# A fused convolution and mixture of experts on Trainium2: rows of up to 4 KB in the dispatch's loads, and three loads at a time

## The chip, the cores and the metric

The kernel runs on one core of one Trainium2 chip. The metric is the device time of one execution in microseconds, the median of the runs of a kernel. Five engines work side by side, each on its own queue of instructions: PE (matrix products), DVE and ACT and POOL (elementwise work), and SP, which here only issues DMA transfers. All transfers run on the core's 16 DMA engines. Before the change the median of 3 runs is 889.47 us (888.85 to 889.73).

## What is computed

A long convolution with a gate, whose result is the input of a mixture of experts with soft routing. Shapes: 4 sequences of 11456 positions and 128 channels, so 45824 tokens of 128 channels; 8 experts of 4 slots each; 1024 hidden features.

```python
h_filt = (np.maximum(pos_emb @ w1, 0.0) @ w2) * window
y = irfft(rfft(x * v) * rfft(h_filt))[:, :S, :]      # along the sequence
x = (x * y).reshape(B * S, D)                        # 45824 x 128

logits = x @ phi                                     # 45824 x 32
d = softmax(logits, axis=0)                          # over the tokens
slot_input = (d.T @ x).reshape(8, 4, 128)
slot_out[e] = np.maximum(slot_input[e] @ moe_w1[e], 0.0) @ moe_w2[e]
c = softmax(logits, axis=1)                          # over the 32 slots
out = c @ slot_out                                   # 45824 x 128
```

## The kernel before

**Convolution.** It is computed as a transform in matrix products, in eight groups of 16 channels. The last step of a group gives gated rows of x, which `p4_out` (L462, L465) and `p4_rest` (L471) store to a scratch tensor `scr` in HBM, channels by tokens. `scr` consists of 16 pieces (`_pieces`), most of them 3296 tokens long; inside a piece each channel is one contiguous row. For the last group the steps run over seven sets of rows, t = 0 to 6, and each stores two pieces.

**Blocks.** The mixture works on 23 blocks: 22 of 16 x 128 = 2048 tokens (1 MB, 8 KB on each of 128 partitions) and one of 768. A block in SBUF has one of 11 places of a ring (`NP`), which are parts of tiles that the convolution has left: `ffw` (blocks 0 to 4), `extra` (block 5), `xreg` and `E`. The token blocks are handled in pairs ("units"), twelve of them.

**Loads of x.** `load` (L695) calls `load_tokens`, which cuts a block where a piece of `scr` ends and then into equal parts of at most `RUN` = 450 tokens, and issues one DMA for each part on SP (L709). A part of 410 tokens is 128 rows of 1640 B. `weights` (L657) loads the first 112 channels of blocks 0 to 5 before the last group's rows exist; `ahead` adds their last 16 channels and loads blocks 6 to 10, each behind the stores of the set t that completes it. Blocks 11 to 22 are loaded by `fetch` inside the mixture: `fetch(i)` loads block i + 11 into the place of block i as soon as block i has been transposed.

**Loads of matrices.** There are 16, of 512 KB: `load_weights` issues each as two halves of 128 rows of 2 KB (L676). Matrices 0 and 1 are loaded by `weights`, the other 14 by `fetch(12)` to `fetch(18)`, two in each place that falls free.

**Order on SP.** DMAs go out in the order in which they stand on SP's queue. The scheduler that lays out the program gives each DMA of SP one of eight semaphores in turn, and a DMA waits until the one eight before it has landed. A DMA into a place also waits until that place has been read.

**Dispatch.** For a unit m the loop does: exponentials of the logits on ACT (`exps`, L849, from the PSUM tile `pl`), transposes of two blocks on PE (L722) and their copies out of PSUM on ACT (L728), the transpose of the weights on DVE (L876), the logits of unit m + 1 on PE (L795), their maxima on DVE (L818, L820), the product with the dispatch weights of unit m - 1 (L890), and the running maximum (L837, L839), which the next exponentials need. PSUM holds two `pl` tiles, one for each block of a unit, so the logits of unit m + 1 overwrite what the exponentials of unit m read.

**Experts and output.** Behind the last unit come the experts: `up` (L1078) with matrices 0 to 7, `turn_hidden` (L1086), `down` (L1096) with matrices 8 to 15. Then each of 24 stretches of tokens is multiplied by the result (L1136), copied and stored (L1144) as 128 rows of up to 8 KB.

Of the kernel before, what the change touches and what calls it, by code (L numbers as in the profile page):

```python
# [17 lines left out]
B, S, D = 4, 11456, 128  # L18
# [27 lines left out]
FF = 1024  # L46
# [592 lines left out]
class Moe:  # L639
# [4 lines left out]
    NP = 2 * XB + 1  # L644
    OB = 4
    CB = 8 * NB
    RUN = 450

    def __init__(self, tc, cp, scr, phi, mw1, mw2, rep, out):
        self.tc, self.cp, self.scr, self.out = tc, cp, scr, out  # L650
        self.phi, self.mw1, self.mw2, self.rep = phi, mw1, mw2, rep

        self.blocks = [(q, min(self.NB, QN - q)) for q in range(0, QN, self.NB)]
        self.xt, self.xq, self.wts = {}, {}, []
        self.pieces = sorted(_pieces().values())

    def weights(self):  # L657
# [14 lines left out]

    def load_weights(self, e, place):
        src = (self.mw1, self.mw2)[e // NEXP][e % NEXP]
        for f in range(0, FF, FF // 2):
            self.tc.nc.sync.dma_start(out=place[:, f : f + FF // 2], in_=src[:, f : f + FF // 2])  # L676
        self.wts.append(place)

    def logit_banks(self):
# [21 lines left out]
    def load_tokens(self, t, z0, z1, d0, d1):  # L701
        for a, m in self.pieces:
            lo, end = max(z0, a), min(z1, a + B * m)
            src = self.scr[D * a : D * (a + B * m)].rearrange("(d t) -> d t", d=D)
            n = max(0, end - lo)
            parts = -(-n // self.RUN) if d0 == 0 else min(n, 1)
            cuts = [lo + n * k // parts for k in range(parts + 1)] if parts else []
            for y0, y1 in zip(cuts, cuts[1:]):
                self.tc.nc.sync.dma_start(out=t[d0:d1, y0 - z0 : y1 - z0], in_=src[d0:d1, y0 - a : y1 - a])  # L709

    def turn(self, pool, tag, i, k0, k1, shared=False):
        nc, inorder = self.tc.nc, self.tc.keep_in_program_order
# [529 lines left out]
def _pieces():  # L1242
    out, t = {}, 0
    for rb in ORDER:
        for h in range(2):
            n = PW - (FULL if rb == 0 and h == 0 else 0)
            out[rb, h] = t, n
            t += B * n
    for h in range(2):
        n = 4 * (R // 8 - LEFT // 8) - 1 + h  # L1250
        out["rest", h] = t, n
        t += B * n
    assert t == TOK
    return out
# [49 lines left out]
```

## Time and profile before

| | |
|---|---|
| median of 3 runs | 889.47 us |
| profiled execution, time | 889.77 us |
| profiled execution, span from first to last instruction | 888.0 us |
| PE busy with products | 855.6 us, 96% of the span |
| DVE, ACT, POOL busy | 715.6, 455.0, 393.2 us |
| DMA moved | 197.04 MB in 108195 packets |
| queue of the instruction fetches for PE | 128 packets, 2.10 MB |

The convolution takes the span up to about 734 us, the dispatch to about 815, the experts to 828, the output the rest. The shares of busy time over the whole span hide this: PE is at 96% in the mean, but in the output it waits for copies and stores. A profile's idle pieces carry the name of what ended them. A wait for several things carries the name of the one that came last by the profile; "issue" means that the engine waited for nothing that the profile shows. DMA share is the mean busy share of the 16 DMA engines.

### The profile page before, as it was taken

Reading aid. Unit: us, or ns where it says so; the run is one execution under the profiler, and the core shown is the slowest. Engines: PE = TensorE matmul, PEld = TensorE weight load, DVE = VectorE, ACT = ScalarE, POOL = GpSimd, SP = SyncE. Lnnn points to the kernel's source line nnn. Section 1 sums busy time; section 2 is a strip of 40 time slices with the busy share of each in tenths; the row PEclk is TensorE's granted clock in tenths of the full one; section 3 lists DMA queues with packets and bytes.
Section 4 is the critical chain, followed back from the end, with each engine's and each line's share of the span. In section 5 each row is a group of like instructions: output and inputs, shape, how many; then the busy total and the mean of one; then the engine's idle time right before and its main releaser. Section 6 shows DMA issues by size and latency. Waiting matters only on the chain. (4 is left out here: it accounts for less than half of the span.)

```text
span 888.0 us, 37632 instructions
## 1 busy us (share of the span) xinstructions
PE 855.6 (96%) x16264; PEld 790.4 (89%) x16264; DVE 715.6 (81%) x1239; ACT 455.0 (51%) x971; POOL 393.2 (44%) x538
## 2 busy tenths in 40 slices
PE   9999999999999999999999999999999999989991
PEld 8998989999999999999999999999999987666540
DVE  5967976899799889989988998899779048886791
ACT  5775558315811751483167128414821637986761
POOL 5003860492078019405910960393079013785750
PEclk9999999999999999999999999999999999999996
DMA  9973775558646754775486476557626978999698
GB/s 317 389 237 109 210 229 173 147 155 268 203 126 200 243 167 133 227 237 172 122 269 201 129 225 207 168 173 229 211 71 186 281 191 271 309 302 327 271 417 372
DMA packets 108195, 197.04 MB, mean 222 GB/s; under 512 B 15865, under 2 KB 71371, under 8 KB 105278
## 3 DMA queue, kind: packets, MB, share of 16 engines
q1 hardware_dynamic: 107854, 194.51, 68.8%
q8 instruction: 128, 2.10, 1.0%
q14 instruction: 37, 0.30, 0.1%
q0 software_dynamic: 32, 0.07, 0.0%
q10 hardware_dynamic: 144, 0.07, 0.0%
HBM read 137.73 MB, written 56.86 MB: 219 GB/s over the span
## 5 line engine op out<-in xcount | busy, mean ns | idle before, releaser
L350 POOL TENSOR_TENSOR T<-m 111x256 f32<-111x256 f32 (+1 forms) x199 | 150.8, 758 | 343.7 <-DVE m L344 343.7
L344 DVE TENSOR_TENSOR m<-p,T 111x1024 f32<-111x1024 f32 (+1 forms) x175 | 200.4, 1205 | 12.7 <-POOL T L351 7.2
L360 PE MATMUL p<-tab,T 111*99 111x112 f32 x2048 | 205.2, 260 | 1.3 <-POOL T L351 0.3
L360 PEld LDWEIGHTS p<-tab,T 111*99 111x99 f32 x2048 | 198.8, 170 | 6.1 <-issue 1.6
L340 PE MATMUL p<-T,W 128*64 128x128 f32 (+1 forms) x3168 | 196.9, 276 | 0.2 <-issue 0.2
L425 ACT ACTIVATE vc<-p 128x412 f32<-128x412 f32 (+1 forms) x112 | 51.7, 513 | 265.3 <-PE p L412 219.4
L340 PEld LDWEIGHTS p<-T,W 128*64 128x64 f32 (+1 forms) x3168 | 182.1, 127 | 2.1 <-issue 0.4
L412 PE MATMUL p<-tab,E 99*64 99x103 f32 (+1 forms) x3584 | 174.1, 252 | 1.2 <-DVE E L373 0.6
L412 PEld LDWEIGHTS p<-tab,E 99*64 99x64 f32 x3584 | 166.4, 136 | 3.3 <-ACT vc L425 0.8
L375 ACT ACTIVATE E<-p 99x448 f32<-99x448 f32 x254 | 131.9, 575 | 63.5 <-PE p L360 57.8
L351 POOL TENSOR_TENSOR T<-m 111x256 f32<-111x256 f32 (+1 forms) x199 | 147.4, 741 | 0.0
L186 ACT ACTIVATE T<-p 128x396 f32<-128x396 f32 x240 | 100.3, 536 | 11.6 <-PE p L174 11.5
L174 PE MATMUL p<-tab1x,x 53*64 53x99 f32 x3648 | 86.7, 246 | 0.2 <-ACT E L224 0.2
L174 PEld LDWEIGHTS p<-tab1x,x 53*64 53x64 f32 x3648 | 79.9, 132 | 4.4 <-ACT E L224 0.4
L443 DVE TENSOR_TENSOR p<-p,vc 128x824 f32<-128x824 f32 (+1 forms) x46 | 47.0, 1022 | 9.9 <-ACT vc L425 9.9
L268 DVE TENSOR_TENSOR x<-x,T 128x448 f32<-128x448 f32 x51 | 31.6, 619 | 22.2 <-DMA x<-in_xf_dram 17.8
L274 DVE TENSOR_TENSOR x<-T 128x224 f32<-128x224 f32 x102 | 39.2, 426 | 1.8
L270 DVE TENSOR_TENSOR T<-x 128x224 f32<-128x224 f32 x102 | 39.2, 426 | 1.7
L224 ACT ACTIVATE E<-fl 111x512 f32<-111x512 f32 (+1 forms) x50 | 26.8, 627 | 21.3 <-PE fl L218 21.3
L451 DVE TENSOR_TENSOR E<-p,E 128x824 f32<-128x824 f32 x36 | 36.6, 1017 | 1.2
L728 ACT ACTIVATE xreg<-pt 128x512 f32<-128x512 f32 (+1 forms) x68 | 35.0, 609 | 2.6 <-PE pt L722 2.5
L344 DVE TENSOR_TENSOR m<-p,E 111x1024 f32<-111x1024 f32 (+1 forms) x25 | 28.7, 1202 | 5.1 <-PE p L340 4.9
(162 smaller groups left out, 970.2 us busy)
## 6 DMA issues: line engine op xcount, KB each, us to landing
x<-in_xf_dram SPq DMA_DIRECT2D x114, 256.0 KB, 4.1
out_dram<-xreg SPq DMA_DIRECT2D x16, 1024.0 KB, 10.3
E<-in_xi_dram SPq DMA_DIRECT2D x37, 412.0 KB, 4.3
T<-in_vf_dram SPq DMA_DIRECT2D x65, 224.0 KB, 4.9
scr<-E SPq DMA_DIRECT2D x67, 206.0 KB, 3.8
T<-hs SPq DMA_DIRECT2D x63, 154.0 KB, 4.5
hs<-E SPq DMA_DIRECT2D x12, 784.0 KB, 4.7
mv<-in_vf_dram SPq DMA_DIRECT2D x42, 224.0 KB, 4.5
```

What stands on the lines that cost most here:

```text
L174: inorder(nc.tensor.matmul(ps[h][RP * d : RP * d + RP, i, s, :], lhsT=sd[js, i, s, d, :], rhs=tab1x[js, J * (s + d) : J * (s + d + 1)], st ...
L186: inorder(nc.scalar.activation(dst, src, AF.Copy))
L270: inorder(eng.tensor_tensor(out=vt[:, :, m : m + 2], in0=xr[:, :, 0:2], in1=xr[:, :, 2:4], op=op))
L340: inorder(nc.tensor.matmul(ps[ns, i].rearrange("p b c -> p (b c)"), lhsT=W[:, k0 + i, ns], rhs=Tf[:, :, k0 + i, :], start=True, stop=True, ...
L344: inorder(nc.vector.tensor_mul(m[:, :n].rearrange("p k s e c i -> p k s (e c i)").rearrange("p k s (b c) -> p k s b c", c=CG), ps[:, :n].u ...
L350: inorder(eng.tensor_tensor(out=Ty[:, 0], in0=m[:, :n, 0, 0], in1=m[:, :n, 1, 1], op=ALU.subtract))
L351: inorder(eng.tensor_tensor(out=Ty[:, 1], in0=m[:, :n, 1, 0], in1=m[:, :n, 0, 1], op=ALU.add))
L360: inorder(nc.tensor.matmul(pk[:, i, 2 * s : 2 * s + 2, :].rearrange("p q r -> p (q r)"), lhsT=T[0:N1, s, 2 * k + i, u // 2, :, u % 2], rhs ...
L375: inorder(nc.scalar.activation(dst, src, AF.Copy))
L412: inorder(nc.tensor.matmul(pv[RP * h : RP * h + RP, 2 * k + i, w, j0:], lhsT=E[:J, r, 2 - 2 * w + s, :], rhs=tab4[:, s, o + j0 : o + NJ], ...
L425: inorder(nc.scalar.activation(vc[:, w, :, j0:], pv[:, :, 0, j0:], AF.Copy, scale=2.0 * w - 1.0))
L443: inorder(nc.vector.tensor_tensor(out=pw[:, :, :, j0:], in1=vc[:, :, :, j0:], op=ALU.add, in0=pw[:, 1:2, :, j0:].to_broadcast([128, 2, 4, ...
```

## The change

`RUN` becomes 1024: a load of x has rows of up to 4 KB, so a whole block loads in two or three parts, depending on where pieces of `scr` end. A matrix is loaded in one DMA of 128 rows of 4 KB. Both kinds go through a new function, `paced`: a load is made to wait until the third paced load before it has landed (`OPEN` = 3). Loads of part of the channels and matrices 0 and 1 are not paced and not counted. The wait is one of SP, which issues the load. Nothing else changes.

```diff
-    RUN = 450
+    RUN = 1024
+    OPEN = 3
...
     def load_weights(self, e, place):
         src = (self.mw1, self.mw2)[e // NEXP][e % NEXP]
-        for f in range(0, FF, FF // 2):
-            self.tc.nc.sync.dma_start(out=place[:, f : f + FF // 2], in_=src[:, f : f + FF // 2])
+        self.paced(self.tc.nc.sync.dma_start(out=place, in_=src), e > 1)
         self.wts.append(place)
...
             for y0, y1 in zip(cuts, cuts[1:]):
-                self.tc.nc.sync.dma_start(out=t[d0:d1, y0 - z0 : y1 - z0], in_=src[d0:d1, y0 - a : y1 - a])
+                self.paced(self.tc.nc.sync.dma_start(out=t[d0:d1, y0 - z0 : y1 - z0], in_=src[d0:d1, y0 - a : y1 - a]),
+                           d0 == 0 and d1 == D)
+
+    def paced(self, load, whole=True):
+        if not whole:
+            return
+        if len(self.open) >= self.OPEN:
+            self.tc.add_manual_dep(load.ins, self.open[-self.OPEN], mybir.DependencyInfo(
+                mybir.DependencyClass.Sync, mybir.DependencyReason.DATA), reason="few loads at a time")
+        self.open.append(load.ins.name)
```

## Rows read from the trace of the kernel before

**Rows 1.** Busy time by stage: window, length, each engine's busy us, clock, DMA.

```profile
core 0: us, PE busy (x) PEld busy (x) DVE busy (x) ACT busy (x) POOL busy (x), PEclk, DMA share, GB/s
640.00:734.00 94.00, 93.12 (x1679) 90.75 (x1679) 56.24 (x68) 33.35 (x71) 39.40 (x60) 1.00 0.66 184
...
756.54:797.35 40.81, 37.49 (x875) 25.95 (x876) 34.85 (x65) 37.27 (x81) 33.42 (x38) 1.00 0.96 309
797.35:815.34 17.99, 16.21 (x397) 12.63 (x396) 13.16 (x32) 12.33 (x31) 9.65 (x8) 1.00 1.00 347
...
828.38:888.00 59.62, 40.34 (x258) 18.89 (x254) 37.95 (x69) 32.43 (x61) 23.79 (x37) 0.88 0.96 394
```

**Rows 2.** Timeline of PE: start, length, line, operation, count [idle before, its releaser].

```profile
756.54 1.92 PE L795 MATMUL pl<-xreg,aux 128*32 128x512 f32 x16 [0.70 <-DMA E<-scr]
...
768.38 0.64 PE L890 MATMUL pa<-E,ev 128*32 128x128 f32 x16 [0.52 <-issue]
...
778.77 1.07 PE L795 MATMUL pl<-ffw,aux 128*32 128x512 f32 x8 [0.75 <-DMA extra<-scr]
...
790.72 0.52 PE L722 MATMUL pt<-aux,extra 64*128 64x64 f32 x9 [0.27 <-issue]
791.17 2.24 PE L795 MATMUL pl<-xreg,aux 128*32 128x512 f32 x16
...
797.59 0.24 PE L837 MATMUL pmt<-rd,aux 128*32 128x8 f32 x5 [1.14 <-issue]
...
808.30 0.49 PE L890 MATMUL pa<-E,ev 128*32 128x128 f32 x9 [0.81 <-issue]
...
813.69 0.52 PE L890 MATMUL pa<-xreg,ev 128*32 128x128 f32 x9 [0.42 <-issue]
```

**Rows 3.** Block 15's last part: its issue on SP; size, us to landing.

```profile
773.12 0.39 SPq L709 DMA_DIRECT2D ffw<-scr  x1
...
ffw<-scr SPq DMA_DIRECT2D x1, 205.0 KB, 5.5
```

**Rows 4.** Timeline of ACT ahead of PE's wait at 756.54.

```profile
755.71 0.69 ACT L849 ACTIVATE et<-pl,xreg 128x512 f32<-128x512 f32 x1 [1.49 <-DVE xreg L839]
```

**Rows 5.** Windows between PE's stalls (counts in brackets), and the queue of instruction fetches.

```profile
768.38:790.72 22.34, 20.65 (x504) 14.84 (x504) 19.19 (x38) 20.59 (x47) 18.67 (x23) 1.00 0.94 299
813.69:823.17 9.48, 9.45 (x120) 4.90 (x124) 2.98 (x23) 5.03 (x8) 3.62 (x7) 1.00 0.61 223
...
q8 instruction: 128, 2.10, 1.0%
```

**Rows 6.** DMA packets begun in 795.3 to 795.4 and in 823.8 to 823.9.

```profile
q8 instruction: 1, 0.02, 60.1%
...
q8 instruction: 1, 0.02, 63.8%
```

**Rows 7.** SP's issue at 781.48, and the packet begun in 781.5 to 781.6.

```profile
781.48 1.96 SPq L709 DMA_DIRECT2D xreg<-scr  x1
...
q8 instruction: 1, 0.02, 97.4%
```

**Rows 8.** The DMA issued at 659.95 with nothing queued: size, us to landing.

```profile
E<-in_xi_dram SPq DMA_DIRECT2D x1, 412.0 KB, 3.0
```

**Rows 9.** SP's issues of blocks 6 and 7.

```profile
734.01 5.91 SPq L709 DMA_DIRECT2D xreg<-scr  x10
```

**Rows 10.** Windows of two single rounds and of seven rounds together.

```profile
759.80:766.34 6.54, 6.44 (x155) 4.47 (x152) 5.75 (x11) 6.54 (x15) 4.89 (x6) 1.00 0.99 328
780.91:787.57 6.66, 6.35 (x157) 4.50 (x153) 5.57 (x12) 6.16 (x15) 5.99 (x8) 1.00 0.88 268
...
752.64:802.23 49.59, 45.33 (x1067) 31.83 (x1064) 42.98 (x80) 43.74 (x97) 36.89 (x40) 1.00 0.95 305
```

**Rows 11.** The last half matrix, in issue at 815.5, and its first product.

```profile
xreg<-in_mw_dram SPq DMA_DIRECT2D x1, 256.0 KB, 5.4
...
823.48 1.93 PE L1096 MATMUL pso<-xreg,E 128*32 128x128 f32 x64
```

More of the change, by code (lines that the diff above doesn't have):

```diff
@@ L653, in __init__ @@
         self.blocks = [(q, min(self.NB, QN - q)) for q in range(0, QN, self.NB)]
-        self.xt, self.xq, self.wts = {}, {}, []
+        self.xt, self.xq, self.wts, self.open = {}, {}, [], []
         self.pieces = sorted(_pieces().values())
```

## The prediction

> **What bounds the kernel now.** I read the busy shares by stage first [rows 1]. Up to 734 us the kernel is the convolution, which the change touches only at its end. From 734 to 815 is the dispatch: its loads bring x back from scr, and PE is busy 37.49 of 40.81 us between 756.54 and 797.35 while the DMA engines are at 0.96, and at 1.00 after that. From 828.38 to the end the output goes out at 394 GB/s with the DMA engines at 0.96: that tail is bound by the stores, it starts with the first store, and nothing of the change is in it. So a microsecond won or lost between 734 and 828 is a microsecond of the whole, and nothing else counts.
>
> Next, PE's own order of time in the dispatch, for what ends its idle pieces [rows 2]. Three kinds are seen. (a) The 0.75 us at 778.77 is put down to a load. Block 15's last piece was issued at 773.12 and took 5.5 us [rows 3], so it landed at 778.6, just ahead of the matmul that reads it: a real load wait. The sixteen logits matmuls at 791.17 took 2.24 us instead of the 1.92 us at 756.54 [rows 2]; I take the 0.32 us in their middle as the same thing. Together 1.07 us. (b) The 0.70 us at 756.54 also carries a load's name, but ACT's exponentials, whose bank these matmuls overwrite, run from 755.71 for 0.69 us [rows 4] and end just before: that one is not the loads'. (c) Five idle pieces are put down to "issue": 0.52, 0.27, 1.14, 0.81 and 0.42 us, in all 3.16 us [rows 2].
>
> What (c) is takes one count. Between the stalls at 768.38 and 790.72 PE ran 504 matmuls and 504 weight loads [rows 5]: with some semaphore instructions that is four times 256. The queue of instruction fetches moved 2.10 MB in 128 packets [rows 5], 16.4 KB each, which over 256 instructions is 64 bytes for one. So PE stalls where a new 16 KB of its program begins, because the fetch, which runs on the same DMA engines, is late. How late: after the boundary at 790.72 the fetch for the next block began at 795.3; after 813.69 the next boundary is 120 matmuls on, at 823.17 [rows 5], and the fetch behind that one began at 823.8 [rows 6], when the loads were done. So 4.6 us when loads are queued and 0.7 us when they are not. SP shows the same moment: an issue that cost 0.39 us at 773.12 [rows 3] took 1.96 us at 781.48, with a fetch beginning at 781.5 [rows 7]. Loads and fetches hold each other up.
>
> **The change part by part.**
>
> Rows. Blocks 6 to 22 now load in 91 pieces of mostly 352 to 448 tokens; with 1024 as the limit, and the pieces of scr still cutting them every 3296 tokens, they are 45, of which 12 have the full 4 KB row, 745 tokens or 2.98 KB in the mean. Cost per row: the three stages give 309/0.96 = 322 GB/s at rows of some 1.5 KB, 347 at 2 KB, 394/0.96 = 410 at 8 KB [rows 1]. Over 16 engines that is 94 ns for a row of 2 KB and 320 ns for one of 8 KB, 0.0367 ns a byte between; 2.98 KB then takes 129 ns, which is 371 GB/s. Blocks 11 to 22 are 11.9 MB: 37 us of the engines' time before, 32 after. They were issued in 40.8 us.
>
> The Trainium skill's "DMA: Bandwidth & Descriptors" (section Specifications) gives 512 B as the least transfer for line rate. By that rule rows of 1.5 KB are long enough, the 371 would stay 322, and (a) would not be won. The three stages disagree, 322 to 410 GB/s, though the last one moves stores.
>
> Pace. Loads of blocks 6 and on and of the last 14 matrices wait on SP for the third one before them. Behind a waiting load stand on SP the later loads, and between 734 and 756 also the stores of the last convolution rows to scr. The price is a rate: three loads in each load's latency l. Blocks 11 to 22 are 32 loads, so they take 32 l / 3. From below, a load of 412 KB alone took 3.0 us [rows 8], and 373 KB is the mean here: 32 us, no more than the rows allow. From above, the 5.5 us of a load behind seven others [rows 3]: 59 us. Break-even with the 40.8 us is l = 3.8 us. Three loads queued are 1.1 MB, which the engines at 371 GB/s move in 3.0 us, so I take l = 3.3 us, nearest to the load alone: 35 us, 5 us earlier by block 22 and about 2 by block 15. That takes away (a), 1.07 us: block 15 was only 0.75 late.
>
> The stores between 734 and 756: the ten pieces of blocks 6 and 7 took SP from 734.01 to 739.92 [rows 9]. Now they are five: three go at once, the fourth when the first has landed, 3.3 us on, and the fifth some 0.5 us later. Even with a start 1.5 us late that is 739.3, so the stores behind them find SP free at 740 as before. Taken at nothing; if the first load lands 2 us late, the stores and what is loaded from them are late by up to 2 us.
>
> Fetches. What queues ahead of a fetch falls from eight loads of some 190 KB to three of 373 KB, and for the matrices from eight of 256 KB to three of 512 KB: to 0.75 of the bytes, to 0.38 of the loads. Which of the two counts, the trace does not say; from below, if only the length of a row counts, nothing is won and it gets worse (below); from above all 3.16 us go. Taking bytes, 4.6 us become 3.6, and stalls of under 1 us go; taking loads, all go. I take two thirds, 2.1 us.
>
> Given back. The loop of logits, maxima on DVE, exponentials on ACT and the next logits has a shortest round: a pair of blocks took 6.54 us and 6.66 us where little waited [rows 10]. The seven rounds from 752.64 to 802.23 took 49.59 us [rows 10]; less their five pieces of (a) and (c), 3.0 us, they would take 6.66 each. That is at the floor, so I give back 0.3 us.
>
> At no cost: the 112-partition preloads of blocks 0 to 5 (15 loads instead of 30) and the two first matrices, unpaced, run before 734, where PE is busy 93.12 of 94.00 us [rows 1]: all their waits together, if they had any, are under 0.9 us. The other matrices: the last landed 5.4 us after its issue near 815.5, so by 820.9, and is read at 823.48 [rows 11]; at three times 512 KB in flight they stay bound by the engines, and start earlier. The cover is 2.6 us, of which PE's gain takes most if they did not.
>
> The sum: -1.1 - 2.1 + 0.3 = -2.9 us. The profiled run is 889.77 us with a span of 888.0; the median is 889.47, and I set the sum against it: **886.6 us**.
>
> **Rivals.**
> - *The loads are won, the fetches are not*: the queue ahead of a fetch is measured in neither bytes nor loads. For it: the bytes hardly fall when three full loads are queued. Then only (a) goes: 888.4.
> - *Nothing moves*: rows do not matter and l comes out at 3.8. For it: DVE's 34.85 and ACT's 37.27 of 40.81 us [rows 1] say that PE is not alone at the limit. 889.5.
> - *Slower: longer rows hold the fetch up.* If a fetch waits for the rows of the one load that an engine is at, eight rows of 1.5 KB are 0.6 us and eight of 4 KB 1.4 us (by the same line, 74 and 170 ns a row): up to 0.8 us more at each of the five boundaries that already stall, +4.0, less 1.1: 892.4. It decides if the wait is a turn and not a queue. Against it: 4.6 us [rows 2, 5, 6] is far more than one turn of 0.6 us. This is what the Trainium skill's "DMA: Bandwidth & Descriptors" (section Queues, rings and completion order) says of the arbitration: an engine goes round its queues and drains a whole packet of several descriptors before it switches. The 4.6 us do not agree with one such packet of 1.5 KB rows.
> - *Slower: the pace starves the engines.* Small pieces (256, 192, 44 and 48 tokens of blocks 12, 16 and 22) hold one of three places, and one engine busy with a fetch holds back a whole load. It decides from l = 3.8 us; at 4.2 the loads take 44.8 us, 4 us more by block 22 and 3 by block 19, which PE waits for: 892.5. The change not doing what it says is a case of this: only 12 of 45 loads have the 4 KB.
>
> **How the numbers follow.** Less than 0.2%, 1.8 us, cannot be told from no change here. The forecast has 0.45 (886.6; of this 0.04 above 887.7), the loads alone 0.22 (888.4, 0.02 of it faster), nothing 0.10, longer rows 0.12, starving 0.11. Faster: 0.41 + 0.02 = 0.43. Same: 0.04 + 0.20 + 0.10 = 0.34. Slower: 0.23. The range goes from all of (a) and (c) won with nothing given back and a little more, 884.8, into the two slower cases, 892.2, which leaves some 2 in 10 outside. The forecast's own range is 885.2 to 887.7.
>
> **What would show it.** Right: no load among the names that PE waits for at the logits; the "issue" pieces of PE between 756 and 815 summing to 1 us; SP's long issues gone; loads of scr landing in 3.0 to 3.6 us; the pairs of blocks at 6.6 us; the first output store at 825.5 and a tail of 59.6 us as now. Wrong: loads of scr landing after 3.8 us and more, or "issue" pieces of over 3 us.

## The result and the profile after

The median of 4 runs is 899.21 us (898.33 to 899.43), beside 889.6 us for the kernel before in the same series (888.85 to 890.28): a ratio of 1.0108, interval 1.0093 to 1.0123. The forecast was 886.6 us with a range up to 892.2. The change made the kernel slower, and by more than its dearest rival.

The first view is of windows again, with the same columns as [rows 1]: busy time of each engine, the granted clock of PE (1.00 is 2.4 GHz, 0.50 is 1.2 GHz), the share of time that the DMA engines were busy, and GB/s. The first line is of the kernel before, from 750 us to its first output store; the others are of the kernel after: the same stretch, its dispatch, the end of the dispatch, the experts, the output.

```profile
750.00:828.38 78.38, 72.57 (x1627) 51.21 (x1620) 58.40 (x132) 61.29 (x135) 54.07 (x60) 1.00 0.85 281
```

```profile
750.00:837.35 87.35, 76.12 (x1620) 54.10 (x1612) 57.44 (x132) 60.82 (x134) 53.43 (x60) 0.94 0.77 250
754.40:802.25 47.85, 42.24 (x969) 29.18 (x960) 39.30 (x74) 41.46 (x92) 35.92 (x39) 0.96 0.85 273
802.25:820.14 17.89, 14.76 (x352) 12.28 (x352) 9.85 (x26) 9.11 (x24) 7.96 (x8) 0.90 0.79 258
820.14:837.35 17.21, 15.31 (x204) 9.76 (x204) 3.96 (x26) 6.69 (x12) 8.50 (x13) 0.90 0.48 167
837.35:897.30 59.95, 40.31 (x258) 18.87 (x254) 37.92 (x69) 32.40 (x61) 23.73 (x36) 0.88 0.95 392
```

The output took 59.95 us instead of 59.62 [rows 1]; the first store came 8.97 us later, so nearly all of the loss lies ahead of it. In that stretch PE was busy 3.55 us longer (76.12 against 72.57) and idle 5.42 us longer (11.23 against 5.81). The DMA engines did less in that time, not more: a share of 0.85 at 273 GB/s in the dispatch, where before they stood at 0.96 and 309, and 258 GB/s at the matrices against 347 [rows 1].

Second view: the waits of PE up to the first store, in us in total, times, and the longest.

```profile
PE pt L731 <- issue: 3.4, 2, 2.8
PE pl L804 <- ACT xreg L737: 3.2, 2, 1.6
PE pl L804 <- DVE rd L829: 1.9, 1, 1.9
PE pso L1105 <- DMA xreg<-in_mw_dram: 1.9, 2, 1.3
PE pl L804 <- ACT et L858: 0.5, 2, 0.3
```

Three waits of `pl` carry the names of ACT and DVE, and no load of x is named. The timeline says otherwise. Here are those three starts on PE, and the issues of SP that fall just ahead of them.

```profile
771.59 1.06 PE L804 MATMUL pl<-ffw,aux 128*32 128x512 f32 x8 [1.62 <-ACT xreg L737]
786.60 1.85 PE L804 MATMUL pl<-xreg,aux 128*32 128x512 f32 x8 [1.91 <-DVE rd L829]
802.50 1.06 PE L804 MATMUL pl<-E,aux 128*32 128x512 f32 x8 [1.57 <-ACT xreg L737]
```

```profile
771.52 0.32 SPq L709 DMA_DIRECT2D ffw<-scr  x1
786.53 0.32 SPq L709 DMA_DIRECT2D xreg<-scr  x1
802.28 0.32 SPq L709 DMA_DIRECT2D ffw<-scr  x1
```

Each of these issues had waited for the third load before it. For the first two, that load's own landing is in the trace: 771.46 and 786.46 us. SP goes on 0.06 us later and PE 0.13 us later: the same landing releases both. For the third the profile has no landing; PE goes on 0.22 us after the issue that waited for it. ACT's copies (L737), which two of the waits are named after, do not hold these products: in the run with four loads at a time (below) the third one's product starts while the copies of that round still run:

```profile
797.68 2.05 ACT L737 ACTIVATE xreg<-pt 128x512 f32<-128x512 f32 x4
798.05 1.04 PE L804 MATMUL pl<-E,aux 128*32 128x512 f32 x8
```

In the run with x paced alone (below), the first two of these products wait for 2.80 and 0.71 us, and there both waits are put down to loads. So these 5.1 us are waits for loads, and with the matrices' 1.9 us the loads cost 7.0 us where they cost 1.07 before.

Third, the granted clock around the second wait, in windows and on PE's timeline.

```profile
780.00:785.00 5.00, 4.64 (x128) 3.51 (x125) 4.64 (x10) 5.00 (x12) 4.69 (x8) 1.00 0.89 276
785.00:790.00 5.00, 3.40 (x38) 1.81 (x40) 3.75 (x8) 2.60 (x5) 4.98 (x4) 0.67 0.89 296
790.00:795.00 5.00, 4.96 (x128) 3.58 (x124) 2.67 (x6) 4.18 (x12) 2.57 (x5) 0.98 0.85 254
...
830.00:835.00 5.00, 4.06 (x64) 3.67 (x65) 0.29 (x1) 0.00 (x0) 2.81 (x5) 0.66 0.04 11
```

```profile
782.37 1.21 PE L731 MATMUL pt<-aux,ffw 64*128 64x64 f32 x32
...
788.38 1.93 PE L731 MATMUL pt<-aux,ffw 64*128 64x64 f32 x32
```

After PE had stood for 1.91 us, 32 transposes of the same form took 1.93 us instead of 1.21: for part of the window the clock stood at its lower level, 1.2 GHz instead of 2.4. The same is seen at 815 to 820 (0.75) and at 830 to 835 (0.66), behind the stalls of 2.79 and 1.30 us. These three windows hold most of the lower clock in the stretch, and so most of the 3.55 us of longer busy time; the kernel before shows 1.00 over its whole stretch. Behind the other two waits for x, of 1.62 and 1.57 us, the clock stayed: it was 1.00 from 770 to 775 and from 800 to 805 us.

### The profile page after: what moved, and what is told of

Read it like the earlier page. It is cut to its first block, busy times and chain, and to the rows that moved or that the text cites. A ratio compares the mean times of both kernels' runs of the same rounds, so it can differ in the third digit from the quotient of the medians.

```text
span 897.3 us, 37472 instructions
## 1 busy us (share of the span) xinstructions
PE 859.2 (96%) x16264; PEld 793.0 (88%) x16264; DVE 714.4 (80%) x1239; ACT 454.9 (51%) x971; POOL 392.6 (44%) x538
## 5 line engine op out<-in xcount | busy, mean ns | idle before, releaser
L737 ACT ACTIVATE xreg<-pt 128x512 f32<-128x512 f32 (+1 forms) x68 | 35.0, 612 | 4.8 <-PE pt L731 4.8
```

The costliest lines, as they stand in the source:

```text
L737: inorder(nc.scalar.activation(dst, pts[h][:, :w], AF.Copy))
```

## The experiments

All times stand beside runs of the kernel before on the same chip. Of the profiled executions, the first output store and the pieces of PE's idle time put down to issue are given where they matter; before they were 828.38 us and 3.16 us.

**The two halves of the change.** Rows of 4 KB and whole matrices without a pace (against the kernel after):

```diff
-    OPEN = 3
+    OPEN = 999
```

> The changed kernel without its pace: rows of up to 4 KB and whole matrices, no load waits for another (up to eight in flight, as before the change). Theory A, the pace starves the DMA engines: the loss goes, 887 to 891 us, and the DMA share between 757 and 797 us is back at 0.95. Theory B, the longer rows are at fault (the engines move them no faster, and each holds back the instruction fetches): it stays slow, 895 us or more, and PE's pieces put down to issue sum to 5 us or more. If both, 892 to 895.

And the pace with the short rows and half matrices of before:

```diff
-    RUN = 1024
+    RUN = 450
...
+        for f in range(0, FF, FF // 2):
+            self.paced(self.tc.nc.sync.dma_start(out=place[:, f : f + FF // 2], in_=src[:, f : f + FF // 2]), e > 1)
```

> The other half of the change: loads cut as before it (rows of up to 450 tokens, half matrices), but three at a time. Starving: a load of 190 KB should take some 2.6 to 2.9 us with three in flight, so 200 to 220 GB/s; blocks 11 to 22, 63 loads, take some 58 us where 41 were: 900 to 912 us, slower than the change as a whole, and PE's waits are for loads. If it is the long rows under the pace that cost, it is 893 us or less.

Measured: rows alone 890.56 us, ratio 1.0031 (1.0018 to 1.0043); pace alone 926.05 us, ratio 1.0423 (1.0401 to 1.0445). So the pace does the harm. The long rows cost some 2 us by themselves, and beside the pace they take some 27 us of its harm back: three pieces in flight hold twice the bytes. The pace alone carried 204 GB/s, as expected, but was dearer than the 900 to 912 us; its granted clock, 0.87 from 750 us to the first store, was not in that sum. Rows alone had theory A's time, and with it the pieces put down to issue, over 5 us, that theory B had. Rows alone, stretches of its loads of x and of its matrices:

```profile
755.80:780.55 24.75, 19.72 (x456) 13.92 (x455) 17.04 (x32) 19.19 (x43) 15.23 (x19) 1.00 1.03 403
780.55:802.40 21.85, 19.16 (x460) 13.83 (x462) 18.53 (x37) 18.68 (x43) 17.63 (x19) 1.00 0.89 331
```

The long rows do what they were costed at, and more: 403 GB/s with a full queue. The last load of x is issued at 779.5 us, before it was 796.0, and no wait for a load is left. But PE is busy only 19.72 of 24.75 us while that goes on. Its timeline says why:

```profile
757.64 0.63 PE L804 MATMUL pl<-xreg,aux 128*32 128x512 f32 x4 [1.69 <-issue]
764.88 0.34 PE L731 MATMUL pt<-aux,xreg 64*128 64x64 f32 x4 [1.86 <-issue]
771.54 0.43 PE L899 MATMUL pa<-E,ev 128*32 128x128 f32 x8 [1.04 <-issue]
...
796.19 0.64 PE L804 MATMUL pl<-xreg,aux 128*32 128x512 f32 x4 [2.21 <-ACT xreg L737]
```

With those at 751.03, 777.87 and 789.94, and the one at 796.19, which sits on the same count of 256 instructions under another name, the late fetches cost 7.8 us. (A boundary is below the place where a new 16 KB of PE's program begins, counted in 256s of its instructions from these stalls.) The fetch for the boundary at 771.54 began 4.2 us after that at 764.88 (the first line shows the packets begun from 769.1 to 769.2 us); when no load was queued, the fetch after the boundary counted at 806.97 began 0.3 us behind it (packets from 807.25 to 807.35):

```profile
q8 instruction: 1, 0.02, 67.8%
...
q8 instruction: 1, 0.02, 80.5%
```

**How many loads at a time.** The number alone changes: one, five, and in a later run four.

```diff
-    OPEN = 3
+    OPEN = 1
```

> The changed kernel with one paced load at a time: it measures a load's time alone and the fetches' lateness with at most one load queued. Both theories have it much slower; Theory A: a load of 512 KB alone takes 3.3 to 3.5 us, 46 of them and the smaller ones make some 150 us where 64 were, so 960 us or so. If a load alone takes 4.5 us or more, three at a time were not starved by being three but by the loads' own length, which is Theory B. The fetches: if what is queued ahead of them makes them late, PE has no stall put down to issue of over 0.3 us in the dispatch.

> The changed kernel with five loads at a time for three. Theory A: three loads in each 4.5 us are some 260 GB/s, five are enough for what the engines can do, so 888 to 892 us. Theory B: the rows are as long as before, so 896 us or more, and a little more than with three, as more is queued ahead of a fetch.

> The change with four loads in place of three, rows up to 4 KB: 1.5 MB in flight, about the 1.4 MB of the kernel before (eight of some 175 KB). If the bytes ahead decide how late a fetch is, its pieces put down to issue sum to 2.5 to 4 us, about the 3.16 of the kernel before, between the 3.4 us of three loads and the 4.6 of five. If the length of the rows decides, they sum to 4.6 us or more, as with five loads and with no pace. For the rate: between the 267 GB/s of three and the 349 of five lie some 310, so the loads' waits are under 3 us, the time 890 to 893. If the time is under 888, four is a size that beats both kernels.

| loads of x at a time | load of x to landing, us (median) | GB/s, DMA share while x loads | loads' waits of PE, us | late fetches, us | fetch behind its boundary, us (mean of seven) | time, us | ratio (interval) |
|---|---|---|---|---|---|---|---|
| 1 | 3.2 | 120, 0.42 | 86.3 | 0 | | 999.53 | one run |
| 3 (the change) | 4.0 | 273, 0.85 | 7.0 | 3.4 | 2.2 | 899.21 | 1.0108 (1.0093 to 1.0123) |
| 4 | 4.9 | 314, 0.93 | 0 | 1.3 | 1.8 | 889.57 | 1.0015 (1.0004 to 1.0026) |
| 5 | 5.3 | 349, 0.98 | 0 | 5.2 | 3.2 | 890.93 | 1.0032 (1.0016 to 1.0048) |
| up to 8 (no pace) | 7.8 | 403, 1.03 | 0 | 7.8 | 3.7 | 890.56 | 1.0031 (1.0018 to 1.0043) |

The late fetches are the pieces put down to issue, and those that fall on the same count of 256 instructions under another name (0.6 us with five loads, 2.2 without a pace). The column behind them is the time from a boundary to the start of the fetch behind it, over the same seven boundaries of the program in each run, which lie between 755 and 797 us; for the kernel before it is 2.8 us. The rate rises with the depth all the way, and from one load to eight so does the latency. With one load nearly all of PE's waits were for loads, and nothing at all was put down to issue. (Its time lies 40 us over what was expected; the granted clock was 0.73 from 756 to 800 us.) The longest lines of that run's view of waits, and the lines of the run with four, each up to the first store:

```profile
PE pl L804 <- DMA xreg<-scr: 31.0, 5, 7.9
PE pl L804 <- DMA ffw<-scr: 21.8, 6, 7.2
PE pso L1105 <- DMA xreg<-in_mw_dram: 8.5, 3, 3.3
PE pl L804 <- DMA E<-scr: 8.2, 2, 4.9
PE ph L1087 <- DMA ffw<-in_mw_dram: 7.2, 4, 2.5
```

```profile
PE pt L731 <- issue: 1.3, 1, 1.3
PE pl L804 <- ACT et L858: 1.3, 3, 0.8
PE pmt L846 <- DVE rd L829: 0.4, 1, 0.4
```

Four loads have rows up to 4 KB and about the bytes in flight of the kernel before (1.5 against 1.4 MB), and less was put down to issue than before, 1.3 against 3.16 us, and less than the 2.5 to 4 us that were expected. With rows of one length, the fetches of x's stretch begin 1.8 us behind their boundaries in the mean with four loads and 3.7 us with up to eight. So it is what is queued ahead of a fetch that makes it late there, and not the length of the rows.

The change itself has one case that does not fit. Behind the boundary counted at 806.0, with three matrices in flight, the fetch began some 4.8 us late (the first line shows the packet begun from 810.7 to 810.8 us), and its longest stall followed:

```profile
q8 instruction: 1, 0.02, 61.1%
...
813.18 0.59 PE L731 MATMUL pt<-aux,E 64*128 64x64 f32 x12 [2.79 <-issue]
```

A later run with the same three matrices in flight and four loads of x had no stall at that boundary. So the number in flight is not the whole account; what else decides was not settled.

Between three and four also lies the rate that PE needs: its waits for loads go from 7.0 us to none. That four is not faster than the kernel before shows in its windows. PE idles 3.5 us up to the first store instead of 5.8, but the granted clock falls around the 1.26 us put down to issue at 807.44, and PE is busy 1.64 us longer:

```profile
750.00:827.74 77.74, 74.21 (x1638) 53.05 (x1634) 59.14 (x133) 62.01 (x139) 54.29 (x60) 0.98 0.81 277
805.00:815.00 10.00, 8.49 (x176) 6.92 (x168) 5.01 (x16) 4.78 (x13) 5.30 (x5) 0.83 0.91 338
```

**Pace on x alone**, the matrices free:

```diff
-        self.paced(self.tc.nc.sync.dma_start(out=place, in_=src), e > 1)
+        self.paced(self.tc.nc.sync.dma_start(out=place, in_=src), False)
```

> The changed kernel with the 14 late matrices not paced (each still one load with rows of 4 KB); the loads of x stay three at a time. Of the 9 us, some 4 were lost ahead of the last unit of the dispatch and some 5 behind it, where the matrices load. Theory A: the matrices' part comes back, 893 to 896 us, and the experts wait for no matrix. Theory B: 899 us, as the rows of the matrices are the same.

Measured: 894.69 us, ratio 1.0081 (1.0058 to 1.0103), first store at 833.88, no wait for a matrix. That is 6.4 us over the kernel before (5.2 to 9.1 by the interval), by the medians two thirds of the change's 9.6; the rest is the matrices' pace, which the forecast had at nothing.

**Whole matrices alone**, in the kernel before:

```diff
-        for f in range(0, FF, FF // 2):
-            self.tc.nc.sync.dma_start(out=place[:, f : f + FF // 2], in_=src[:, f : f + FF // 2])
+        self.tc.nc.sync.dma_start(out=place, in_=src)
```

> The kernel before with one edit: an expert's matrix goes as one load with rows of 4 KB instead of two halves; x as before, no wait. Theory (bytes ahead of the fetch set its lateness): the line behind block 12 holds 512 KB loads instead of 256 KB ones, the fetches between 797 and 815 us start 3.5 us or more after their boundaries instead of 2.7 to 3.2, their stalls rise from 2.4 us to 3 to 5, time 889 to 891 beside 888 to 889. Rival (fewer bytes-in-pieces, the matrices end sooner and the late stalls go with the queue): stalls under 1.5 us, 886 to 888.

Measured: 890.35 us, ratio 1.0019 (1.0005 to 1.0033), the first store at 829.78. One stall of 1.54 us at 808.96 is put down to issue, fewer than the theory had, so neither expectation fits whole; what is new is the granted clock around it, 0.83 over ten microseconds in which the DMA engines moved 408 GB/s:

```profile
805.00:815.00 10.00, 8.17 (x200) 6.97 (x198) 5.49 (x13) 5.84 (x17) 5.71 (x5) 0.83 1.02 408
```

**Four of x, a shallower line of matrices.** The number becomes an argument of `paced`: four for x; three whole matrices in the first run, six halves in the second (its edit stands behind the mark).

```diff
+        self.paced(self.tc.nc.sync.dma_start(out=place, in_=src), e > 1, 3)
...
+        for f in range(0, FF, FF // 2):
+            self.paced(self.tc.nc.sync.dma_start(out=place[:, f : f + FF // 2], in_=src[:, f : f + FF // 2]), e > 1, 6)
```

> Four loads of x at a time, three matrices, rows up to 4 KB. With four of both the rest of the loss sat at the matrices: 1.26 us put down to issue at 807 us and a granted clock of 0.83 between 805 and 815 us. If the line of four matrices (2 MB) makes that, three make it 0.5 us or less and the clock stays 1.00: 886 to 888. If the three matrices come too slowly instead (three of 512 KB moved at 258 GB/s in the change), the last lands after 823 us and PE waits for matrices in the experts: 889 to 892.

> Four loads of x at a time with rows up to 4 KB; the matrices as halves of 256 KB with rows of 2 KB, six at a time, the same 1.5 MB as three whole ones. If bytes alone count, as the run with three whole matrices, within 1 us. If more and shorter pieces in flight carry more (347 GB/s with eight of them in the kernel before), the last matrix lands 2 us or more earlier than there, with the same stalls: 886 to 888.

Measured: 889.13 us, ratio 1.0009 (0.9991 to 1.0027), and 888.40 us, ratio 0.9997 (0.9982 to 1.0013). The medians lie 0.7 us apart, as the case of bytes alone had it. The profiled execution with six halves lost nothing to loads and has no piece put down to issue, kept its clock, and stored first at 824.47 us, 3.9 us ahead of the kernel before. Its window from 750 us and its waits (of the 2.3 us, one of 1.41 at 757.06 falls on the count of 256 and ends 0.7 us after the exponential that it is named after, so a late fetch may be part of it):

```profile
750.00:824.47 74.47, 71.36 (x1624) 51.49 (x1620) 58.49 (x132) 61.02 (x135) 53.92 (x60) 1.00 0.85 284
```

```profile
PE pl L804 <- ACT et L858: 2.3, 4, 1.4
PE pmt L846 <- DVE rd L829: 0.4, 1, 0.4
```

That execution took 886.12 us; the twelve of that kernel lie between 885.11 and 893.6, and the 23 of the kernel before in the same series between 885.58 and 891.9. So this profile is of one of its quicker executions, the kernel before has such ones too, and the medians, 888.40 against 888.48, show no gain. With the three whole matrices PE waited for matrices in the experts (2.4 us), as that run's second case had it. No version beat the kernel before by more than its interval.

**Loads of half the height.** Rows of 4 KB, each load of x and each matrix as two of 64 partitions, no pace (the part for x, against rows alone):

```diff
+                for p0, p1 in ((0, 64), (64, 128)) if whole else ((d0, d1),):
+                    self.tc.nc.sync.dma_start(out=t[p0:p1, y0 - z0 : y1 - z0], in_=src[p0:p1, y0 - a : y1 - a])
```

> Rows of up to 4 KB without a pace, each load cut in two of 64 partitions: the rows of the run with the rows alone, but half the bytes in a load, so with eight in flight about the bytes of the kernel before (1.5 MB, and 2.1 MB of matrices). If a fetch is late by the bytes queued ahead of it: PE's stalls at the ends of its 16 KB fall from 7.8 us there to 3 or 4 us, and 887 to 889 us. If it is late by the length of the rows: still 6 to 8 us of stalls, and 890 us or more.

Measured: 913.74 us, ratio 1.0287 (1.0259 to 1.0315). By its letter the second expectation holds, with 7.8 us put down to issue. But the loss is far beyond both, PE waited for loads as well, and the run does not settle its question, because the engines carried less at the same share:

```profile
756.00:812.00 56.00, 47.23 (x1060) 33.24 (x1056) 41.60 (x79) 43.27 (x95) 35.35 (x39) 0.94 1.02 247
```

**Loads behind PE's work instead of behind landings.** A load of block i + LEAD waits for the transposes of block i; the matrices stand behind blocks 14 to 20. LEAD is 7, then 4 and 5 with the matrices spread, then 4 with the short rows; in the last, short rows up to block 15, long ones and LEAD 7 above.

```diff
+        if mo.NP <= i + mo.LEAD < NBL:
+            mo.load(i + mo.LEAD, w=i)
...
+                self.behind(self.tc.nc.sync.dma_start(out=t[d0:d1, y0 - z0 : y1 - z0], in_=src[d0:d1, y0 - a : y1 - a]), i)
+                i = None
```

> A version to beat both: rows of up to 4 KB, no wait for landings; instead the load of block i + 7 waits on SP until PE has transposed block i, and two matrices each wait for the transposes of blocks 14 to 20. So a block is loaded for each block worked on, 1 MB in some 3.3 us where the engines need 2.6, and little is queued. If both the starving and the queue ahead of the fetches are the causes: no wait of PE for a load, stalls at the ends of PE's 16 KB of 1.5 us or less, 885 to 887 us. If the fetches are late for another reason: 887 to 889 us.

> Rows up to 4 KB, whole matrices, no wait for a landed load. The load of block i+4 waits for the PE transposes of block i, where the run gated at block i+7 kept six to eight loads in flight; the matrices go out one, one, two, two, two, three, three behind blocks 14 to 20. Theory (the lateness of PE's instruction fetches is the line of bytes ahead of them): with about three loads in flight a fetch starts 1.5 to 3 us after its 256-instruction boundary instead of 3.6 to 4.7; the issue stalls fall from 6 to under 3 us, the load waits stay under 1 us, time 885 to 888. Rival one (the 4 KB row itself holds the fetch up): fetches still start 3.5 us or more behind, stalls over 4.5 us, 889 to 892. Rival two (three loads in flight can't carry the 276 GB/s that the blocks take, whatever gates them): waits for loads of 1.5 us or more at every fourth block as with the pace, 893 or more.

> The same with the load of block i+5 behind the transposes of block i. Theory: about four loads in flight, fetches start 2.5 to 4 us after their boundaries, issue stalls 3 to 5 us, no load wait, 887 to 890. Rival one: as with one block less, stalls over 4.5 us. Rival two: the waits for loads are gone with one more block of lead, and the time falls below that of the run with four.

> As the run with four blocks of lead, but with the short rows (450 tokens at most) and the half matrices of the kernel before. Theory: a shallow line again, so fetches start under 3 us behind their boundaries; but 309 GB/s is all that the short rows carried with the line full, and under 276 with it shallow, so the blocks wait for loads: 3 to 10 us of waits, 891 to 898. Rival (the length of the rows has no part in it, a load issued early enough is there in time at either length): within 1.5 us of the run with long rows and four blocks of lead.

> An attempt to have both: blocks 0 to 15 load with the short rows of before, blocks 16 and up with rows up to 4 KB, each behind the PE transposes of the block seven earlier; whole matrices behind blocks 14 to 20 (one, two, two, two, two, two, three). Theory: the line is that of before up to 775 us and shallow from there to 795 us, PE is busy for 9.9 of 10 us there as in the gated runs, and only the matrices' stalls are left (2 to 3 us): 885 to 888. Rival (what is not loaded early has to be loaded late): the time saved in the shallow stretch comes back as stalls and a lower granted clock between 795 and 815 us, 889 to 892.

Measured, in this order: 891.45 us, ratio 1.0040 (1.0026 to 1.0053); 897.23, 1.0095 (1.0075 to 1.0115); 895.71, 1.0079 (1.0061 to 1.0096); 903.47, 1.0162 (1.0147 to 1.0177); 893.21, 1.0054 (1.0031 to 1.0077). These five do not test what was expected of them. The edit gives the wait to the first piece of a block only (`i = None`), which left the other pieces, and those of later blocks, free to go ahead of it on SP. In the last run block 16's first piece, 96 KB, was issued at 776.20, after pieces of the blocks behind it, and landed 9.2 us later; PE stood for it until 785.45, again under another name, and the granted clock was 0.69 over the ten microseconds from 785:

```profile
785.45 1.94 PE L802 MATMUL pl<-extra,aux 128*32 128x512 f32 x8 [4.09 <-ACT E L870]
```

The 14.25 us that the short rows lost at 778.19 and the 3.52 of LEAD 5 at 768.12 are waits put down to loads, too. What can be used of these runs is a stretch: once the early pieces were in, the run with LEAD 4 had PE busy 9.95 of 10 us, with its loads at 187 GB/s:

```profile
785.00:795.00 10.00, 9.95 (x278) 8.07 (x278) 9.27 (x20) 9.97 (x22) 9.69 (x12) 1.00 0.62 187
```

## Why the prediction was wrong

**What bounds the kernel: right.** The tail changed by 0.33 us, and the 8.97 us by which the first store came later are nearly all of the loss.

**The five stalls: right in kind.** Fetches of 16 KB behind queued loads: one load at a time leaves none, a full queue of long rows makes them 7.8 us. That fewer loads ahead would take them away held while x loads: with three at a time none falls between 756 and 802 us. But the 2.1 us of the sum did not come, 3.16 us became 3.4, and 2.79 of them lie at 813.18, in the matrices. The 4.6 us that the prediction took for "when loads are queued" was also the longest case: the eleven fetches of the kernel before between 755 and 814 us began 0.9 to 4.6 us behind their boundaries.

**The cost of a row: right, and kept out of use.** 371 GB/s was worked out, 403 were measured with the queue full. The Trainium skill's "DMA: Bandwidth & Descriptors" (section Specifications) gives 512 B as the least transfer for line rate, by which rows of 1.5 KB would be as good as longer ones; the traces do not agree, with 309 GB/s at a share of 0.96 in [rows 1] and 403 at 1.03 here. But the change's queue was never full.

**The pace: the step that failed.** The latency was taken at 3.3 us, "nearest to the load alone". Measured, the loads of x whose landings the trace has took 4.0 us in the median and 4.2 in the mean, over the 3.8 that the prediction itself named as a sign of being wrong. The rate came out lower still. The first of the 32 loads of blocks 11 to 22 went out at 754.40 and the first matrix behind them at 803.16: 48.8 us, where before it was 40.8 [rows 1], and 35 were forecast. By the prediction's formula, 32 l / 3, that is l = 4.6 us; the rival's 4.2 us and 44.8 us were nearer, and still too low. So they started 2.1 us earlier than before and ended 5.8 us later. Above the break-even the kernel got slower, as it was to; the choice between the bounds was wrong. 3.0 us came from a load with nothing beside it, 5.5 from one behind seven shorter ones, and the forecast took three loads to fill the engines at 371 GB/s. With three in flight they moved 273 at a share of 0.85: part of the engines stood idle while a load waited to be issued.

**The rival's own size.** It had 3 us lost by block 19, for 892.5. The waits for x alone were 5.1 us. The rest was in no term: 3.55 us of longer busy time, at the lower clock behind waits of 1.30 to 2.79 us, and the matrices.

**The matrices at no cost: wrong.** They were to "stay bound by the engines, and start earlier". They started at 803.16 instead of 797.35, moved at 258 GB/s instead of 347, and PE waited 1.9 us for the last ones. The cover of 2.6 us in [rows 11] was gone through the same mistake.

**The longer rows hold the fetch up: rejected as a mechanism.** Four loads at a time with the same rows lost less to issue than the kernel before, and their fetches began 1.8 us behind the boundaries instead of 2.8. The 2 us of rows alone go with the depth: up to eight loads of these rows in flight are some 3.1 MB (403 GB/s by 7.8 us) instead of 1.4.

**Open.** Each sum of stalls is of one profiled execution, and the executions of one kernel lie up to 9.6 us apart, so a difference of a microsecond or two between such sums shows nothing by itself. Why a fetch behind three matrices was as late as one behind a full queue of x was not settled, nor whether six halves beside four loads of x can be had faster than before: that run's profiled execution was, by 3.6 us, and its median was not.

## What to carry to other kernels

A limit on the loads in flight is a rate: loads in flight times their size, divided by the latency at that number, which is not the latency of a load alone. Size it from the rate that the consumer needs, and measure the latency at that depth; here three were too few, four just enough for PE to wait for no load, and eight only made other traffic wait. No depth made this kernel faster than it was. When a wait carries the name of an instruction that does not hold the product, look for the landing of a load just before its end.

## What the runs showed of the hardware

- Latency against loads of x in flight (rows up to 4 KB, some 370 KB in the mean): 3.2, 4.0, 4.9, 5.3 and 7.8 us with one, three, four, five and up to eight; 120, 273, 314, 349 and 403 GB/s.
- A fetch of 16 KB of instructions started 0.3 us after its boundary with nothing queued, 4.2 us after it behind a full queue of loads of x, and once 4.8 us after it with three matrices in flight.
- A wait of PE can cost twice: behind 1.91 us the granted clock was 0.67 over 5 us. Not every wait did it: in the run with rows alone PE stood for 1.86 us at 764.88, and its granted clock was 1.00 from 755.80 to 780.55. Around a wait of 1.30 us at 830.94 it was 0.66.
- Rows of 4 KB to 64 partitions at a time moved at 247 GB/s with a share of 1.02, to 128 partitions at 403 with 1.03.
